# Layer 1 of a channel mixer by seven products of quarters in place of eight, from the fourth chunk on

## The chip, the cores and the metric

One core of one Trainium2 chip. The metric is device microseconds of one execution; the time before is the median of three runs. Engines: PE does matmuls, DVE (VectorE), ACT (ScalarE) and POOL (GpSimd) work elementwise, SP mostly issues DMAs. Each works off its own queue in order.

## The reference

Attention over 32 memory slots for 8 batches x 8 heads, 576 tokens of 64 channels; then a mixer over tokens and one over channels (512 channels, 1536 hidden):

```python
a = exp(phi - max over tokens) ; a /= sum over tokens
k_m, v_m = a^T k, a^T v                      # 32 slots by 64
attn = softmax(q k_m^T / 8)                  # 576 by 32
x    = attn v_m                              # 8 x 576 x 512 after joining the heads
u    = x + (relu(x^T w_tok1) w_tok2)^T       # tokens, d_tok = 256
out  = u + relu(u w_ch1) w_ch2               # channels, d_ch = 1536
```

Products keep float32's accuracy: an operand is split into a high part in the matmul's shorter format (`float32r`, by a cast on ACT) and the rest, the low part (by a subtraction on DVE or POOL), and a product is three matmuls: high x high, high x low, low x high.

## The kernel before

The 8 x 576 rows of `u` are cut into nine *chunks* of 512 columns (columns are tokens here, since everything is held transposed). For a chunk, `u` is 4 groups of 128 channels by 512 columns, in `uh` and `ul`. The hidden layer has 12 blocks of 128 (`f`). Layer 1 of a block, `mm_1`, is 4 channel groups x 3 = 12 matmuls of 512 columns into a PSUM tile `cp` (two of them in turn); then ACT writes the relu's high part (`high`, tile `hh`) and DVE its low part (`low`, tile `hl`). Layer 2 of a block, `ch2`, is 4 output groups x 3 = 12 matmuls into `acc0` to `acc3`, which are summed over all blocks and added to `u` on DVE (`add`), after POOL has put `uh + ul` into `o` (`residual`).

The weights `c1h`, `c1l` (layer 1) and `c2` (layer 2) stay in SBUF for the whole run. After a first part that a planner orders (chunk 0, with the conversion of the weights), the rest is written out as a loop over blocks: each step is layer 1 of block f, then layer 2 of block f-1. Time is counted in half-steps `h`, two a block, 24 a chunk. `at(h, fn)` puts other work at a half-step: heads in sets of four (`Quad(b, Q)`, two a batch), each set with

- `phi_max`, `phi_exp`, `phi_sum` (softmax over tokens), then at `m` `step_kv` (matmuls `kvp`, and small DVE work), `values`,
- at `r+2` `step_s` (matmuls `sp`, then on DVE two transposes, a maximum, a subtraction, and an exp on ACT: `sm1`), at `r+3` `sm2` (sum, reciprocal, product, transpose into `aT` on DVE, then a CAST `a` on ACT, its low part on POOL),
- at `r+6` `nat` and `r+7` `v_pairs` (casts `nat` and four `vv` on ACT, lows on DVE), `r+8` `step_A`, `r+9` `step_R` (token mixer), from `r+10` `step_u` (matmuls `u`, four tiles), whose results go into the chunks' `uh`/`ul`, and for columns of a later chunk into `rest`, from where `take` fetches them.

A step's work on ACT and DVE stands in those engines' queues between the relus of the blocks, in the order in which it is written.

Of the kernel before, what the change touches and what calls it, by code (L numbers as in the profile page):

```python
# [15 lines left out]
ALU = mybir.AluOpType  # L16
# [12 lines left out]
def kernel(  # L29
# [44 lines left out]
    REST = S - CW  # L74

# [34 lines left out]
    c1h = wp.tile([P, NKK, FF], F32R, name="c1h")  # L110
    c1l = wp.tile([P, NKK, FF], F32R, name="c1l")
# [25 lines left out]
    class Chunk:  # L137
        def __init__(s, c):
            s.c, s.n, s.hid = c, f"_{c}", {}
            s.uh = wide(F32R, "uh" + s.n)  # L140
            s.ul = wide(F32R, "ul" + s.n)

# [5 lines left out]
        def mm_1(s, ps, f):  # L148
            w = slice(f * P, (f + 1) * P)
# [10 lines left out]
        def high(s, ps, f):  # L160
            if s.c < CHUNKS - 1 or f < NF - 4:
                h = sb.tile([P, CW], F32R, tag="hh", name=f"hh{f}" + s.n, bufs=2)
                l = sb.tile([P, CW], F32R, tag="hl", name=f"hl{f}" + s.n, bufs=2)
            else:
                if f == NF - 4:
                    s.stay = [
                        sb.tile([P, 4, CW], F32R, tag=t, name="stay" + t, bufs=1)
                        for t in ("rest", "kv")
                    ]
                h, l = (t[:, f - NF + 4] for t in s.stay)  # L170
            s.hid[f] = (h, l)
            relu_high(h, ps)
# [4 lines left out]
        def ch2(s, f):  # L177
            if f == 0:
                s.acc = [
                    pacc.tile([P, CW], F32, tag=f"acc{a}", name=f"acc{a}" + s.n)  # L180
                    for a in range(NKK)
                ]
            s.end = NF - (3 if s.c == CHUNKS - 1 else 0)
            for a in range(NKK):
                s.second(s.acc[a], a, [f], 0, s.end)
# [32 lines left out]

    chunks = {}

    def mixer(c):
        if c not in chunks:
            chunks[c] = Chunk(c)
        return chunks[c]

# [3 lines left out]
    class Quad:  # L229
# [63 lines left out]
        def step_kv(s):  # L293
            s.kvp = pch.tile([P, CW], F32, tag="ch", name="kvp" + s.n)
# [271 lines left out]
        def u_high(s, ps, db, hf):  # L566
# [6 lines left out]
            if n:  # L573
                nc.scalar.copy(out=mixer(s.b).uh[:, kk, to], in_=ps[:, :n])  # L574

        def u_low(s, ps, db, hf):
            kk, (n, to) = 2 * s.Q + db, s.own(hf)
            ch = mixer(s.b)
            if n:
                nc.vector.tensor_tensor(  # L580
                    out=ch.ul[:, kk, to], in0=ps[:, :n], in1=f32(ch.uh[:, kk, to]), op=ALU.subtract
                )
# [112 lines left out]
    class PartC1:  # L695
# [13 lines left out]
        def dst(s):  # L709
            return c1h[:, :, s.w], c1l[:, :, s.w]  # L710
# [874 lines left out]
    beside = {}  # L1585
    for b in range(2, B):
        for Q in range(2):
            qd = second if b == 2 and not Q else Quad(b, Q)
            r = 2 * NF * b - (14 if Q else 26)
            if b == 2 and not Q:  # L1590
                r = m = 2 * NF
            else:

                m = r - (0 if b == 2 else 10 if b > 3 or Q else 8)
                at(max(m - 11, 2 * NF), qd.load_phi)
                at(m - (6 if (b, Q) == (3, 0) else 7), qd.phi_max, k=1)
                at(m - (3 if b == 2 else 4), qd.phi_exp, k=1)
                at(m - (2 if b == 2 else 3), qd.phi_sum, k=1)
                at(loaded + 1, qd.load_kv, k=1)
                at(r - 4, qd.load_q, k=1)  # L1600
            loaded = m
            at(m, qd.step_kv)
            at(m + 4, qd.values)
            if b > 2:
                at(m + 3, qd.get_keys, k=1)
            else:
                at(m + 1, qd.step_T)
            at(r + 2, qd.step_s)
            if Q or b == 2:
                at(r + 3, qd.sm2)  # L1610
            else:
                beside[r + 3] = qd
            at(r + (3 if qd is second else 4), qd.a_pair, 1)
            at(r + 6, qd.nat, k=1)
            at(r + 7, qd.v_pairs)
            at(r + 8, qd.step_A)
            at(r + 9, qd.step_R)
            for x in range(4):
                at(r + 10 + x // 2 * (1 if qd is second else 2), qd.step_u, x // 2, x % 2)
        at(2 * NF * (b - 1) + 7, lambda b=b: mixer(b).take(), k=1)  # L1620
    for c in range(CHUNKS):
        h = 2 * NF * (c + 1)
        if c:
            at(h - (4 if c < CHUNKS - 1 else 8), lambda c=c: chunks[c].residual(), k=1)
        if c == CHUNKS - 1:
            break
        sums = [lambda c=c, x=x: chunks[c].add(x) for x in range(NKK)]
        if h + 1 in beside:
            qd = beside.pop(h + 1)
            sums = [sums[0], qd.S_sum, *sums[1:], qd.S_mul, qd.sm3]  # L1630
        for fn in sums:
            at(h + 1, fn, k=-1)
        at(h + 3, lambda c=c: chunks[c].store(), k=1)
    at(2 * NF * (B - 1) + 7, lambda: mixer(B).take(), k=1)
# [9 lines left out]
    for g in range(NF, NF * CHUNKS):  # L1644
# [6 lines left out]
        if c < CHUNKS - 1 or f < NF - 3:  # L1651
            before[0].ch2(before[1])
# [3 lines left out]
    assert not events and not beside  # L1656

    last = chunks[CHUNKS - 1]
    last.ch2(NF - 4)
# [94 lines left out]
```

## Time and profile before

| | |
|---|---|
| median of 3 runs | 765.95 us (765.69 to 766.15) |
| profiled execution | 765.61 us, span 763.8 us |
| PE / DVE / ACT / POOL busy | 99% / 47% / 32% / 18% of the span |
| granted PE clock | 1.0 throughout |
| HBM | 55.51 MB read, 13.89 MB written, 91 GB/s over the span |

Columns of a row that groups instructions: line, engine, operation, out<-in by the program's names (buffer numbers left out), partitions x elements, count | busy us, mean ns of one | idle time of the engine before them, and what ended it. In order of time: start us, duration us, engine, line, operation. A wait's row: who <- for whom: us in total, times, longest. The busy share of PE says little, since a matmul's listed time overlaps the next one's; distances of starts tell its pace.

### The profile page before, as it was taken

The page shows a single profiled execution, that of the slowest core. Times are in us where ns is not written, and L with a number is a line of the kernel's source. Part 1 is how long each engine was busy: PE and PEld are TensorE (multiplying, and loading weights), DVE is VectorE, ACT ScalarE, POOL GpSimd, SP SyncE. Part 2 cuts the span into 40 slices and gives each one's busy share as a digit, 9 for nine tenths or more (in the row PEclk, how much of TensorE's full clock was granted, in tenths as well). Part 3 has the DMA queues.
Part 4 walks back from the last instruction along what each step waited for, and adds up shares of the span by engine and source line. Part 5 has one row for each costly group of instructions (what it writes and reads, how often), then busy time and mean ns, then how long its engine had stood idle before and what let it go on. Part 6 is the DMA issues. An engine that isn't in the chain of part 4 may idle for free.

```text
span 763.8 us, 11121 instructions
## 1 busy us (share of the span) xinstructions
PE 757.0 (99%) x4514; PEld 631.2 (83%) x4514; DVE 362.3 (47%) x612; ACT 245.2 (32%) x477; POOL 139.8 (18%) x118
## 2 busy tenths in 40 slices
PE   9999999999999999999999999999999999999998
PEld 8777788787878888888888787888888888888886
DVE  4989874657354434545264535543442412212113
ACT  5897553333213231323233221413232312111010
POOL 2144343002311022101310131102310402002000
PEclk9999999999999999999999999999999999999999
DMA  9954630432215040605033220604040101001001
GB/s 357 416 198 157 227 103 10 122 143 65 90 18 192 12 143 1 189 21 154 0 86 123 61 94 15 195 6 149 1 123 0 32 1 56 0 1 56 0 1 55
DMA packets 58178, 70.11 MB, mean 92 GB/s; under 512 B 38416, under 2 KB 48016, under 8 KB 53904
## 3 DMA queue, kind: packets, MB, share of 16 engines
q1 hardware_dynamic: 57696, 68.76, 27.3%
q8 instruction: 35, 0.57, 0.3%
q10 hardware_dynamic: 432, 0.66, 0.2%
q14 instruction: 15, 0.12, 0.1%
HBM read 55.51 MB, written 13.89 MB: 91 GB/s over the span
## 4 chain that ended last, share of the span: by engine, by line
PE 92%; DVE 3%; DMA 2%; ACT 1%; issue 1%; POOL 0%; SPq 0%; ACTq 0%; POOLq 0%
PE cp L158 37%; PE acc L191 36%; PE u L555 8%; PE Ap L515 3%; PE kvp L297 2%; PE u L1213 2%; PE Rp L534 1%; PE sp L393 1%; PE end L191 1%; DMA raww<-in_w_tok_dram 1%; DVE rawc L639 1%; DMA raw<-rows 1%; DVE rawc L622 0%; POOL w1l L650 0%; PE Ap L1188 0%
## 5 line engine op out<-in xcount | busy, mean ns | idle before, releaser
L191 PE MATMUL acc<-hh,c 128*128 128x512 f32 x832 | 276.4, 393 | 0.0
L128 DVE SCALAR_TENSOR_TENSOR hl<-cp,hh 128x512 fp32r<-128x512 f32 x104 | 71.7, 689 | 263.3 <-ACT hh L125 263.2
L191 PEld LDWEIGHTS acc<-hh,c 128*128 128x128 f32 x832 | 156.2, 188 | 37.0 <-issue 4.2
L158 PE MATMUL cp<-uh,c1h 128*128 128x512 f32 x432 | 163.1, 391 | 0.0
L158 PE MATMUL cp<-ul,c1h 128*128 128x512 f32 x432 | 162.4, 390 | 0.0
L191 PE MATMUL acc<-hl,c 128*128 128x512 f32 x416 | 162.3, 390 | 0.0
L158 PE MATMUL cp<-uh,c1l 128*128 128x512 f32 x432 | 162.2, 389 | 0.0
L125 ACT ACTIVATE hh<-cp 128x512 fp32r<-128x512 f32 x104 | 62.0, 596 | 260.8 <-PE cp L158 260.7
L158 PEld LDWEIGHTS cp<-uh,c1l 128*128 128x128 f32 x432 | 81.1, 188 | 17.1
L158 PEld LDWEIGHTS cp<-ul,c1h 128*128 128x128 f32 x432 | 81.1, 188 | 16.4
L158 PEld LDWEIGHTS cp<-uh,c1h 128*128 128x128 f32 x432 | 80.8, 188 | 16.6 <-issue 0.5
L191 PEld LDWEIGHTS acc<-hl,c 128*128 128x128 f32 x416 | 78.2, 188 | 14.1
L203 POOL TENSOR_TENSOR o<-uh,ul 128x512 f32<-128x512 f32 x36 | 48.8, 1383 | 115.3 <-PE cp L158 46.9
L457 POOL TENSOR_TENSOR a<-aT,a 64x576 fp32r<-64x576 f32 x22 | 31.4, 1430 | 183.1 <-ACT a L456 115.9
L456 ACT CAST a<-aT 64x576 fp32r<-64x576 f32 x24 | 16.1, 672 | 56.6 <-DVE aT L430 56.3
L251 DVE TENSOR_REDUCE pr<-phi 128x128 f32<-128x640 f32 x22 | 29.0, 1322 | 10.5 <-ACT phi L275 7.3
L555 PE MATMUL u<-w2l,Rh 128*128 128x288 f32 x112 | 33.1, 295 | 0.0
L555 PE MATMUL u<-w2h,Rh 128*128 128x288 f32 x112 | 33.0, 295 | 0.0
L555 PE MATMUL u<-w2h,Rl 128*128 128x288 f32 x112 | 32.9, 294 | 0.0
L284 POOL PARTITION_ALL_REDUCE psr<-pr x11 | 11.9, 1081 | 88.5 <-issue 56.3
L128 DVE SCALAR_TENSOR_TENSOR Rl<-Rp,Rh 128x512 fp32r<-128x512 f32 x14 | 9.7, 690 | 35.8 <-ACT Rh L125 35.8
L580 DVE TENSOR_TENSOR ul<-u,uh 128x288 fp32r<-128x288 f32 (+8 forms) x48 | 16.9, 356 | 18.9 <-ACT uh L574 18.6
(196 smaller groups left out, 875.1 us busy)
## 6 DMA issues: line engine op xcount, KB each, us to landing
kv<-in_kv_dram SPq DMA_DIRECT2D x12, 1280.0 KB, 6.9
rawc<-in_w_ch_dram SPq DMA_DIRECT2D x12, 1024.0 KB, 10.0
q<-in_q_dram SPq DMA_DIRECT2D x16, 576.0 KB, 5.7
out_dram<-o SPq DMA_DIRECT2D x8, 1024.0 KB, 7.5
phi<-in_phi_dram SPq DMA_DIRECT2D x16, 320.0 KB, 3.8
rows<-S SPq DMA_DIRECT2D x56, 72.0 KB, 2.0
kv<-in_kv_dram SPq DMA_DIRECT2D x6, 640.0 KB, 8.8
raw<-rows SPq DMA_DIRECT2D x14, 256.0 KB, 2.9
```

Source lines behind the costliest of these rows:

```text
L125: nc.scalar.activation(out=h, in_=ps, func=AF.Relu)
L128: nc.vector.scalar_tensor_tensor(out=l, in0=ps, scalar=0.0, in1=f32(h), op0=ALU.max, op1=ALU.subtract)
L158: nc.tensor.matmul(ps, l[:, a, w], r[:, a], start=n == 0, stop=n == len(mm) - 1)
L191: nc.tensor.matmul(ps, l_[f // 2][:, f % 2, a * P : (a + 1) * P], r[:, w], start=f == start and x == 0, stop=f == end - 1 and x == 2,)
L203: nc.gpsimd.tensor_tensor(out=s.o[:, a], in0=f32(s.uh[:, a]), in1=f32(s.ul[:, a]), op=ALU.add)
L251: nc.vector.tensor_reduce(out=m.rearrange("p (i m) -> p i m", i=4), in_=s.pt.rearrange("p i j m -> p i m j"), axis=AX.X, op=op,)
L297: nc.tensor.matmul(s.kvp[32 * i : 32 * i + 32, : 2 * D], s.pt[:, i, j, :], s.kv[:, :, j, i, :], start=j == 0, stop=j == NC - 1,)
L456: nc.scalar.copy(out=h, in_=s.aT[own])
L457: s.low_eng.tensor_tensor(out=l, in0=s.aT[own], in1=f32(h), op=ALU.subtract)
L515: nc.tensor.matmul(ps[:, :TT], a, w, start=x == 0, stop=x == len(mm) - 1)
L555: nc.tensor.matmul(ps[:, :HALF], a, r, start=x == 0, stop=x == len(mm) - 1)
L580: nc.vector.tensor_tensor(out=ch.ul[:, kk, to], in0=ps[:, :n], in1=f32(ch.uh[:, kk, to]), op=ALU.subtract)
```

## The change

Chunks 3 to 8 (`WIN = 3`) do layer 1 by Winograd's form of Strassen's scheme. The 512 channels are cut in two halves, the 512 columns in two (`HW = 256`), and two hidden blocks are taken together (a *pair*): a 2 x 2 by 2 x 2 product of quarters, with seven products in place of eight. One product is 2 channel groups x 3 = 6 matmuls of 256 columns. Six pairs make a chunk; `f` advances by two, four half-steps a pair.

- *Sums of u* (`Quarters`): T1 to T4, four DVE operations of 512 elements a chunk, then highs on ACT and lows on DVE for the seven right sides (`early_1` to `late_4`, in the last 13 half-steps before the chunk). `u` itself stays whole in float32, and the chunk's output is added into it; `residual` falls away.
- *Sums of weights* (`Sums`): in chunks 1 and 2, for each of six pairs, two DVE additions of 512, four of 256, a cast of 1024, a subtraction of 1024; eight DMAs on SP's queue store them with the plain quarters in device memory. In chunks 3 to 8 each pair loads four *units* from there (`load_unit`, on ACT's queue, 512 KB, the fourth 256 KB), two ahead of their use (`AHEAD`). The SBUF of `c1h`, `c1l` becomes twelve tiles for weights, units, sums and results.
- *Products*: two PSUM tiles, `qa` and `qb`, take turns; a sum over products is partly kept in PSUM (T2, T3, T4 go onto what `qa` has), partly made by ACT copies and DVE additions in the tile `c`. After each of the first six products stands a slice of layer 2 of the pair before (three matmuls of 512), after the seventh two.
- The relus: two of 512 on ACT and two on DVE a pair become, on ACT, four copies of 256, two relus of 256 and one of 512; on DVE three additions of 256, two lows of 256 and one of 512.
- The sets of heads come every 12 half-steps, up to six half-steps earlier; the last set ends at half-step 161 of 216. `sm2` of each set stands at `r+3` as one piece (before, it was partly mixed with the chunk's `add`). `kvp` moves from the PSUM pool of `cp` to that of the heads.
- `end`, the last piece of layer 2, has two blocks for three.

```diff
+    HW = CW // 2
+    WIN, AHEAD = 3, 2
...
+        def late_1(s):
+            for name in ("21", "T2", "T3"):
+                s.rooms(name)
+            s.mixed("T3", "22", "12", ALU.subtract)
+            s.mixed("T2", "T3", "11", ALU.add)
+            s.mixed("T4", "21", "T2", ALU.subtract)
+            s.part_high("21", "T2", "T3")
...
+        def product(s, ps, weights, name, first, end):
+            mm = [
+                (l[:, a], r[:, a])
+                for a in range(2)
+                for l, r in (
+                    (weights[:, 0], s.x[name][0]),
+                    (weights[:, 0], s.x[name][1]),
+                    (weights[:, 1], s.x[name][0]),
+                )
+            ]
...
+    def load_unit(n):
...
+        t = sb.tile([P, 1024], F32R, tag="c1", name=f"unit{n}", bufs=NF)
...
+        m = 512 if j == 3 else 1024
+        nc.scalar.dma_start(out=f32(t)[:, :m], in_=sums[p].to[:, j, :m])
...
-            r = 2 * NF * b - (14 if Q else 26)
...
+    starts = [(2, 0, 24, 24), (2, 1, 34, 34), (3, 0, 38, 44), (3, 1, 48, 54), (4, 0, 58, 64)]
+    while starts[-1][:2] != (B - 1, 1):
+        b, Q, m, r = starts[-1]
+        starts.append((b + Q, 1 - Q, r + 4, r + NF))
...
+    for x, h in zip(sums, (4, 9, 14, 24, 29, 34)):
+        for y, fn in enumerate((x.words, x.sum, x.low)):
+            at(2 * NF * (WIN - 2) + h + y, fn, k=1)
...
+        def product(ps, k, name, first):
+            if not k % 2:
+                load_unit(n + k // 2 + AHEAD)
+            ch.product(ps, units[n + k // 2][:, k % 2], name, first, name in ("21", "22", "T4"))
...
+        a = tile("qa")
+        product(a, 0, "11", True)
+        run(h - 1, 1)
+        out(et[:, t0], a)
+        mix()
+        b = tile("qb")
+        product(b, 1, "21", True)
+        add(et[:, t0], b[:, :HW], et[:, t0])
+        run(h, 0)
+        mix()
+        run(h, 1)
+        product(a, 2, "T2", False)
+        out(et[:, t1], a)
+        run(h + 1, -1, 0)
+        mix()
+        product(b, 3, "T1", True)
+        mix()
+        out(ot[:, t0], b)
+        run(h + 1, 1)
+        product(a, 4, "T3", False)
+        out(ot[:, t1], a)
+        add(ot[:, t1], ot[:, t0], ot[:, t1])
+        relu_high(oh[:, t1], ot[:, t1])
+        relu_low(oh[:, t1], ol[:, t1], ot[:, t1])
+        run(h + 2, 0)
+        mix()
+        run(h + 2, 1)
+        product(b, 5, "22", False)
+        add(et[:, t1], b[:, :HW], et[:, t1])
+        relu_high(eh, et)
+        relu_low(eh, el, et)
+        mix()
+        run(h + 3, -1, 0)
+        product(a, 6, "T4", False)
+        relu_high(oh[:, t0], a[:, :HW])
+        relu_low(oh[:, t0], ol[:, t0], a[:, :HW])
+        mix(2)
```

Where the queues stand at the places that matter, in the program's order (names end with batch and set, or with the chunk, and a serial number):

DVE at the softmax of set (5, 1), before: the heads' rows, then the lows of blocks 7 and 8.

```order
L419 TENSOR_REDUCE sm_5_1_4024<-S_5_1_3966 128x18
L420 TENSOR_SCALAR sm_5_1_4024<-sm_5_1_4024 128x18
L421 RECIPROCAL sm_5_1_4024<-sm_5_1_4024 128x18
L424 TENSOR_TENSOR S_5_1_3966<-S_5_1_3966,sm_5_1_4024 128x576
L430 STREAM_TRANSPOSE aT_5_1_4037<-S_5_1_3966 128x576
L128 SCALAR_TENSOR_TENSOR hl7_4_4061<-cp7_4_4045,hh7_4_4060 128x512
L128 SCALAR_TENSOR_TENSOR hl8_4_4095<-cp8_4_4078,hh8_4_4094 128x512
```

The five rows of `sm2` stand ahead of the low part of block 7.

DVE there now (`c1` is the pair's result tile, `qhl13` and `qal12` low parts):

```order
L570 STREAM_TRANSPOSE S_5_1_4296<-sp1_5_1_4287 128x288
L577 TENSOR_REDUCE mx_5_1_4299<-S_5_1_4296 128x18
L580 TENSOR_TENSOR S_5_1_4296<-S_5_1_4296,mx_5_1_4299 128x576
L1851 TENSOR_TENSOR c1_4_4195<-qb1_4_4210,c1_4_4195 128x256
L129 SCALAR_TENSOR_TENSOR qal12_4_4192<-c1_4_4195,qal02_4_4191 128x512
L589 TENSOR_REDUCE sm_5_1_4318<-S_5_1_4296 128x18
L590 TENSOR_SCALAR sm_5_1_4318<-sm_5_1_4318 128x18
L591 RECIPROCAL sm_5_1_4318<-sm_5_1_4318 128x18
L594 TENSOR_TENSOR S_5_1_4296<-S_5_1_4296,sm_5_1_4318 128x576
L600 STREAM_TRANSPOSE aT_5_1_4331<-S_5_1_4296 128x576
L129 SCALAR_TENSOR_TENSOR qhl13_4_4194<-qa1_4_4196,qhh03_4_4193 128x256
```

The heads' rows are the same; the last row, which reads `qa` out, stands behind all of them, as `hl7` did.

ACT at the same place, before:

```order
L125 ACTIVATE hh6_4_3952<-cp6_4_3939 128x512
L415 ACTIVATE S_5_1_3966<-S_5_1_3966 128x576
L456 CAST a0_5_1_4039<-aT_5_1_4037 64x576
L125 ACTIVATE hh7_4_4060<-cp7_4_4045 128x512
L456 CAST a1_5_1_4040<-aT_5_1_4037 64x576
```

The relu of block 7 stands behind the first CAST of `a`.

And now ACT from the softmax to the next pair:

```order
L585 ACTIVATE S_5_1_4296<-S_5_1_4296 128x576
L126 ACTIVATE qal02_4_4191<-c1_4_4195 128x512
L626 CAST a0_5_1_4333<-aT_5_1_4331 64x576
L392 DMA unit33_4337<-sums2_1328 128x1024
L126 ACTIVATE qhh03_4_4193<-qa1_4_4196 128x256
L392 DMA unit34_4359<-sums2_1328 128x1024
```

The relu that reads `qa` comes after the CAST of `a`, as `hh7` did, and after a unit's load.

PE from the seventh product of that pair on (one row per slice or product, x6 for six matmuls):

```order
L327 MATMUL qa1_4_4196<-xT4_4_3988,unit31_4246 128x256 x6
L184 MATMUL acc2_4_4255<-qhh01_4_4027,c20_500 128x512
L184 MATMUL acc2_4_4255<-qhl11_4_4028,c20_500 128x512
L184 MATMUL acc2_4_4255<-qhh01_4_4027,c20_500 128x512
L184 MATMUL acc3_4_4265<-qhh01_4_4027,c20_500 128x512
L184 MATMUL acc3_4_4265<-qhl11_4_4028,c20_500 128x512
L184 MATMUL acc3_4_4265<-qhh01_4_4027,c20_500 128x512
L327 MATMUL qa2_4_4358<-x_4_3556,unit32_4274 128x256 x6
L184 MATMUL acc0_4_4206<-qal02_4_4191,c22_638 128x512
L184 MATMUL acc0_4_4206<-qal12_4_4192,c22_638 128x512
L184 MATMUL acc0_4_4206<-qal02_4_4191,c22_638 128x512
L327 MATMUL qb2_4_4371<-x21_4_3874,unit32_4274 128x256 x6
```

In PSUM the new `qa2` is in the room of `qb1`, and `qb2` in that of `qa1`, so PE waits for the read-out of `qa1` ahead of `qb2`. Before, 24 matmuls of 512 columns stood between layer 1 of a block and the first use of its low part:

```order
L158 MATMUL cp7_4_4045<-ul_4_3107,c1h_98 128x512
L158 MATMUL cp7_4_4045<-uh_4_3106,c1l_99 128x512
L191 MATMUL acc0_4_3699<-hh6_4_3952,c26_852 128x512
L191 MATMUL acc0_4_3699<-hl6_4_3953,c26_852 128x512
L191 MATMUL acc0_4_3699<-hh6_4_3952,c26_852 128x512
```

After the last row of `cp7` come layer 2 of block 6 and layer 1 of block 8, and only then `hl7` is read.

ACT at `nat` and `v_pairs` of that set, before:

```order
L121 CAST nat_5_1_4114<-raw_5_1_4034 128x512
L121 CAST nat_5_1_4114<-raw_5_1_4034 64x128
L465 CAST vv_5_1_4119<-vh_5_1_3736 64x128 x4
L125 ACTIVATE hh9_4_4141<-cp9_4_4124 128x512
L121 CAST Ah_5_1_4160<-Ap_5_1_4145 128x256
```

One relu of a block follows the six casts. ACT there now:

```order
L122 CAST nat_5_1_4464<-raw_5_1_4328 128x512
L122 CAST nat_5_1_4464<-raw_5_1_4328 64x128
L126 ACTIVATE qhh04_4_4353<-c2_4_4357 128x512
L635 CAST vv_5_1_4481<-vh_5_1_4075 64x128 x4
L392 DMA unit37_4486<-sums3_1329 128x1024
L126 ACTIVATE qal05_4_4355<-qa2_4_4358 128x256
```

The four casts of `vv` and a unit's load now stand between two relus of the same pair, and the second of these reads `qa` out.

More of the change, by code (lines that the diff above doesn't have):

```diff
@@ L175, in low, with ch2 @@
             relu_low(*s.hid[f], ps)
[L177 to L184, printed above, removed]
+        def ch2(s, f, channels=range(NKK)):
+            for a in channels:
+                if f == 0 and a == 0:
+                    s.acc = {}
+                if f == 0:
+                    s.acc[a] = pacc.tile([P, CW], F32, tag=f"acc{a}", name=f"acc{a}" + s.n)
                 s.second(s.acc[a], a, [f], 0, s.end)
@@ L1621 @@
-    for c in range(CHUNKS):
-        h = 2 * NF * (c + 1)
[L1623 to L1633, printed above, removed]
@@ L1658 @@
+    for c in range(WIN, CHUNKS):
+        for p in range(NF // 2):
+            quarters(c, p)
+    run(2 * NF * CHUNKS - 1, 1)
+    assert not events
     last = chunks[CHUNKS - 1]
-    last.ch2(NF - 4)
-    for a in range(NKK):
-        last.add(a)
     banks = [(pat, "at", 2)] * 2 + [(pacc, f"acc{a}", 1) for a in range(3)]
```

260 lines of the change are left out of this document (200 added, 60 removed).

## The prediction

> **What bounds the kernel now.** I read the page first (span, busy shares, the chain that ended last), then the waits of PE, then single instructions in order of time, on PE for the pace of a matmul and on DVE and ACT where the heads' softmax falls.
>
> ```profile
> span 763.8 us, 11121 instructions
> PE 757.0 (99%) x4514; PEld 631.2 (83%) x4514; DVE 362.3 (47%) x612; ACT 245.2 (32%) x477; POOL 139.8 (18%) x118
> ...
> PE 92%; DVE 3%; DMA 2%; ACT 1%; issue 1%; POOL 0%; SPq 0%; ACTq 0%; POOLq 0%
> PE cp L158 37%; PE acc L191 36%; PE u L555 8%; PE Ap L515 3%; PE kvp L297 2%; PE u L1213 2%; PE Rp L534 1%; PE sp L393 1%; PE end L191 1%; DMA raww<-in_w_tok_dram 1%; DVE rawc L639 1%; DMA raw<-rows 1%; DVE rawc L622 0%; POOL w1l L650 0%; PE Ap L1188 0%
> ```
>
> PE is the bound: its instructions make 92% of the chain, layer 1 (`cp`) 37% of the span. The two longest waits of PE in the whole run are these; both lie in the first 150 us, and the others are shorter:
>
> ```profile
> PE pp L892 <- POOL mask L89: 1.6, 1, 1.6
> PE pp L943 <- DVE ul L580: 0.5, 1, 0.5
> ```
>
> So the time is the matmuls' pace, as long as nobody makes PE wait. A matmul's listed duration overlaps the next one's; the pace is the distance of starts:
>
> ```profile
> 303.58 0.39 PE L158 MATMUL cp<-uh,c1h 128*128 128x512 f32 x1
> ...
> 304.49 0.39 PE L158 MATMUL cp<-ul,c1h 128*128 128x512 f32 x1
> 758.32 0.28 PE L191 MATMUL end<-staykv,c 128*128 128x256 f32 x1
> ...
> 759.04 0.28 PE L191 MATMUL end<-staykv,c 128*128 128x256 f32 x1
> ```
>
> Four matmuls of 512 columns take 0.91 us, 0.227 each; six of 256 take 0.72 us, 0.120 each.
>
> **Term 1, the seven products.** Per pair of hidden blocks 24 matmuls of 512 (5.45 us) become 42 of 256 (5.04 us): 0.41 us less. Six chunks of six pairs are 36 pairs: **-14.7 us**. An eighth of the columns is gone, but 18 more matmuls each bring some 13 ns that don't shrink (0.120 less half of 0.227, doubled). The Trainium skill ("TensorE: Matmul & The Clock Gate", Back-to-back issue gap) gives N/2.4 + 2.5 ns instead, 216 and 109 ns; by it the term would be -21 us and the sum 6 us lower; the rows disagree with its fixed part, and the measurement decides.
>
> **Where the time goes instead: the room before PE must wait.** In the old order layer 1 of block f is followed by layer 2 of f-1 and layer 1 of f+1, 24 matmuls or 5.45 us, before layer 2 of f needs the relu's low part. The trace uses that room at every softmax:
>
> ```profile
> 506.52 0.72 PE L393 MATMUL sp<-q,kb 64*32 64x288 f32 x16
> 507.17 1.30 PE L297 MATMUL kvp<-kv,phi 128*32 128x128 f32 x40
> 508.40 0.50 PE L191 MATMUL acc<-hh,c 128*128 128x512 f32 x1
> 507.32 0.69 DVE L128 SCALAR_TENSOR_TENSOR hl<-cp,hh 128x512 fp32r<-128x512 f32 x1 [6.42 <-ACT hh L125]
> 507.93 0.84 DVE L400 STREAM_TRANSPOSE S<-sp 128x288 f32<-128x288 f32 x2
> ...
> 509.59 0.76 DVE L410 TENSOR_TENSOR S<-S,mx 128x576 f32<-128x576 f32 x1
> ...
> 512.22 0.73 DVE L419 TENSOR_REDUCE sm<-S 128x18 f32<-128x576 f32 x1
> ...
> 514.29 0.78 DVE L430 STREAM_TRANSPOSE aT<-S 128x576 f32<-128x576 f32 x1
> 516.31 0.69 DVE L128 SCALAR_TENSOR_TENSOR hl<-cp,hh 128x512 fp32r<-128x512 f32 x1 [1.23 <-ACT hh L125]
> 506.69 0.60 ACT L125 ACTIVATE hh<-cp 128x512 fp32r<-128x512 f32 x1 [5.11 <-PE cp L158]
> 510.38 0.69 ACT L415 ACTIVATE S<-S 128x576 f32<-128x576 f32 x1 [3.09 <-DVE S L410]
> 515.11 0.68 ACT L456 CAST a<-aT 64x576 fp32r<-64x576 f32 x1 [4.04 <-DVE aT L430]
> 515.69 0.59 ACT L125 ACTIVATE hh<-cp 128x512 fp32r<-128x512 f32 x1
> ```
>
> ACT reads `cp` 0.17 us after PE moved on (506.69 against 506.52). The next `hh` stands behind the CAST of `a` and starts at 515.69, its `hl` ends at 517.00, and still no wait of PE is listed. In the new order the seventh product's tile `qa` must be read out by ACT and DVE before the *second* product of the next pair may write into it (its first goes into the tile of `qb`, free earlier). Between lie two slices of layer 2, one product and one slice: 1.36 + 0.72 + 0.68 = 2.76 us. And before that reading, in the queues, stand `sm2` on DVE, and the CAST of `a` and a unit's load on ACT (the first two places of the order above).
>
> More durations:
>
> ```profile
> L209 DVE TENSOR_TENSOR o<-end,o 128x256 f32<-128x256 f32 x2 | 0.8, 425 | 1.0 <-PE end L191 1.0
> L122 DVE TENSOR_TENSOR nat<-raw,nat 128x512 fp32r<-128x512 f32 x12 | 8.4, 700 | 12.6 <-ACT nat L121 12.3
> L122 DVE TENSOR_TENSOR nat<-raw,nat 64x128 fp32r<-64x128 f32 x12 | 4.4, 367 | 0.5 <-ACT nat L121 0.2
> L121 ACT CAST Ah<-Ap 128x256 fp32r<-128x256 f32 x12 | 4.5, 372 | 12.6 <-PE Ap L515 12.6
> L465 ACT CAST vv<-vh 64x128 fp32r<-64x128 f32 x48 | 14.2, 296 | 0.4
> L121 ACT CAST nat<-raw 128x512 fp32r<-128x512 f32 x12 | 7.5, 621 | 12.5 <-DMA raw<-rows 12.3
> L121 ACT CAST nat<-raw 64x128 fp32r<-64x128 f32 x12 | 3.5, 294 | 0.6 <-DMA raw<-rows 0.6
> q<-in_q_dram SPq DMA_DIRECT2D x16, 576.0 KB, 5.7
> raw<-rows SPq DMA_DIRECT2D x14, 256.0 KB, 2.9
> L247 SPq DMA_DIRECT2D q<-in_q_dram x14: 328/334/536, 18.6 to 566.2; - x14
> DMA to landing us min/median/max: 3.7/5.7/13.5
> ```
>
> (The last row is that of `q`.) A product is 6 x 0.120 = 0.72 us, a slice (three matmuls of 512) 0.68, `sp` 0.65 (506.52 to 507.17), `kvp` 1.23.
>
> **Term 2, the softmax (`step_s` at r+2, `sm2` at r+3).** Clock 0 is the end of the fifth product. PE itself needs `sp` 0.65, slice, product, slice, product, two slices, product, slice: 6.21 us to the next pair's second product. The queues: copy by ACT 0.17 + 0.37, add on DVE 0.43, half a relu 0.37 and its low part 0.43: 1.77. Transposes to the subtraction (507.93 to 510.35) 2.42: 4.19. Exp 0.69: 4.88, beside it the add of the sixth product. Relu of 512 0.60: 5.48, low part 0.69: 6.17. `sm2` (512.22 to 515.07) 2.85: 9.02. CAST of `a` 0.68: 9.70, issue of the unit 0.33: 10.03, half a relu 0.37 and low part 0.43: 10.83. With 0.04 us at some seven hand-overs (515.07 to 515.11), 11.1. PE waits 11.1 - 6.2 = 4.9 us. Seven sets of heads have their `sm2` in the new chunks (r = 76, 88, ... 148): **+34.3**.
>
> **Term 3, `nat` and `v_pairs` (r+6, r+7), one pair later.** No `sp` here: PE needs 5.56. Copy, add, half a relu 1.34; both casts of `nat` 2.26; DVE has the lows at 2.66 and 3.03, its add at 3.45; relu 4.05; four casts of `vv` 1.18: 5.23; unit 0.33, half a relu 0.37, low part 0.43: 6.36, with hand-overs 6.5. PE waits 0.95, seven times: **+6.7**.
>
> **Term 4, chunk edges.** `late_1` falls right behind `sm2` for three chunks and puts three casts of 0.62 ahead of the copy that the third product waits for: some 0.35 us each, **+1**.
>
> **What costs nothing, and its cover.** A pair without heads' work: from the sixth product's end the add, relu and low part take 0.17 + 0.43 + 0.60 + 0.69 = 1.9 us, needed after 3.5; the seventh product's relu takes 0.17 + 0.37 + 0.43 = 1.0 of 2.76. DVE rises from 1.4 to some 2.8 us a pair, ACT from 1.2 to 2.8 and 1.3 for four issues, of 10.5 us. u's sums and splits (11 of 0.70 on DVE, 7 of 0.62 on ACT a chunk, less the lows of u that fall away) go into such pairs. POOL loses `residual` there, which nobody waited for. Earlier heads leave the last chunks without them: no PE time. Fewer blocks in `end` only move matmuls.
>
> The weights' sums put about 26 us on DVE (6 x (2 x 0.70 + 4 x 0.43 + one of 1024, twice 0.60 to 0.70) = 26) into chunks 1 and 2, and eight DMAs each on SP's queue ahead of `kv`, `q` and `rows`.
>
> ```profile
> 100.00:200.00 100.00, 99.53 (x638) 83.62 (x637) 58.41 (x96) 33.67 (x74) 21.27 (x16) 1.00 0.31 99
> ```
>
> DVE was busy 58 of these 100 us, the room there is the old 5.45, SP is idle most of the time: 0, at most a wait of 1 us at each, 6.
>
> **Units.** Each is 512 KB on ACT's queue. The tightest is issued after the relu behind the sixth product, 1.2 us after it, and needed 5.56 after it: 4.4 us. No row shows such a load; by `q` (576 KB, fastest 3.7) and `raw` (256 KB, 2.9) it lands in some 3.5, by `q`'s median 5.7. `q` shares its queue with `kv` ahead of it, which units don't, so I take 0; the other end is 36 x 1.3 = 47 us. Nothing below zero is possible here, the old kernel had no such loads.
>
> **Sum.** 765.6 (the profiled execution: span 763.8 and 1.8 around it, 0.3 below the median of the runs) - 14.7 + 34.3 + 6.7 + 1.0 = **793**.
>
> **Rivals.**
> - *Faster: the softmax doesn't hold `qa`.* The gain stands and the time is 751. It needs PE's wait for a set of heads to stay under 14.7 / 7 = 2.1 us. Against it: DVE's own rows between `sp` and the second product, 2.42 + 0.43 + 0.69 + 2.85 + 0.43 = 6.8, already pass PE's 5.56 without any of ACT's. For it: that these rows stand one behind the other I read from the order alone, and no run has shown such a wait yet. 13%.
> - *The clock falls in the waits.* PE has no gap like 4.9 us before. At the start, after rest, PE ran slower:
>
> ```profile
> 1.56 4.97 PE L892 MATMUL pp<-ident 128*128 128x128 f32 x30 [1.56 <-POOL mask L89]
> 7.68 2.62 PE L892 MATMUL kp<-ident 128*128 128x128 f32 x22
> ```
>
>   166 ns a matmul against 119: 1.4 us lost over 30. Seven waits would each pay that again: 793 + 10 = 803. The same page of the Trainium skill (Why this matters for your kernels) says that a gap of some 3 us can halve the clock; here only the start bears on it. 20%.
> - *Units land late*, as `q`'s median: 793 + 47 = 840. 7%.
> - *The waits are a third to a half of that*, because PE comes late to these places anyway: 765 to 772. 5%.
>
> My own forecast, 786 to 800, has 55%. The range takes in the clock's case, the six us of the weights' sums, part of the late units and the halved waits: 768 to 822. What this kernel's measurement can tell from no change is about 0.2%, 1.5 us. Faster 0.14 (the first rival and a little of the last), within it 0.03, slower 0.83.
>
> **What the new profile would show.** Matmuls of `qa` and `qb` 0.120 us apart. PE's waits lead with `qb` on DVE's low part of the relu, seven times near 5 us, between some 400 and 700 us; ACT's CAST of `a` just ahead of the half relu; the chain with DVE and ACT well above 3% and 1%; the last two chunks without waits. If `qa` or `qb` waits on DMA of `unit` in nearly every pair, the units' term is wrong; if PE's waits sum to less than 15 us, Term 2 is.

## The result, and the profile after

The changed kernel takes 821.08 us, median of 4 runs (819.54 to 821.39), against 766.05 for the one before beside it: a ratio of 1.0715, 95% interval 1.0697 to 1.0734. It is 55 us slower; 27 were forecast. The profiled execution took 819.54 us, its span is 817.8, its mean granted clock 0.979.

The page's head, and the chain that ended last:

```profile
span 817.8 us, 13215 instructions
PE 771.7 (94%) x5159; PEld 660.4 (81%) x5159; DVE 469.7 (57%) x840; ACT 322.7 (39%) x699; POOL 110.5 (14%) x94
...
PE 41%; DMA 9%; DVE 7%; ACT 3%; issue 1%; SPq 0%; ACTq 0%; DVEq 0%
```

The shares are of the whole span, but this chain can be followed back only to 307 us, so they add up to 62%. Of that part PE makes about two thirds (41 of 62), DMA a seventh, DVE a ninth; before, the chain reached back to the start and PE made 92% of it. So DMA, DVE and ACT have come onto the path. PE's busy 94% hides part of that, since matmuls at half the clock count as busy for twice as long. PE's waits (who waits <- for whom: us in total, times, longest), the longest rows, that of the start left out:

```profile
PE qb L327 <- DVE qhl L129: 24.5, 7, 3.6
PE qa L327 <- DMA unit<-sums: 5.8, 6, 1.7
PE qb L327 <- DVE qal L129: 3.3, 7, 0.5
...
PE acc L184 <- DVE qal L129: 1.0, 6, 0.2
PE acc L184 <- DVE hl L129: 0.8, 1, 0.8
```

The first is Term 2, seven times; the third Term 3. The first of the seven in order of time (start us, duration us, engine, line, operation; [idle before <- releaser]), from the end of the fifth product:

```profile
327.96 0.72 PE L563 MATMUL sp<-q,kb 64*32 64x288 f32 x16
...
331.38 0.76 DVE L580 TENSOR_TENSOR S<-S,mx 128x576 f32<-128x576 f32 x1
...
333.41 0.69 DVE L129 SCALAR_TENSOR_TENSOR qal<-c,qal 128x512 fp32r<-128x512 f32 x1 [0.94 <-ACT qal L126]
333.62 1.27 PE L184 MATMUL acc<-qal,c 128*128 128x512 f32 x3
334.02 0.74 DVE L589 TENSOR_REDUCE sm<-S 128x18 f32<-128x576 f32 x1
...
336.10 0.78 DVE L600 STREAM_TRANSPOSE aT<-S 128x576 f32<-128x576 f32 x1
336.92 0.67 ACT L626 CAST a<-aT 64x576 fp32r<-64x576 f32 x1 [3.54 <-DVE aT L600]
337.49 0.37 ACT L126 ACTIVATE qhh<-qa 128x256 fp32r<-128x256 f32 x1
337.90 0.42 DVE L129 SCALAR_TENSOR_TENSOR qhl<-qa,qhh 128x256 fp32r<-128x256 f32 x1 [1.02 <-ACT qhh L126]
338.38 0.58 PE L327 MATMUL qb<-x,unit 128*128 128x256 f32 x1 [3.49 <-DVE qhl L129]
```

PE is done with the slice of layer 2 at 334.89 and stands still until 338.38. All that time the half relu that reads `qa` (337.49) waits behind the CAST, and the CAST behind `sm2` on DVE.

What came on top is the clock. Busy time in seven stretches just after these waits began (us: busy and count of PE, PEld, DVE, ACT, POOL; granted PE clock; DMA share; GB/s):

```profile
337.10:343.90 6.80, 5.52 (x50) 4.52 (x51) 2.75 (x10) 1.81 (x4) 2.81 (x2) 0.50 0.87 236
388.30:391.70 3.40, 3.40 (x38) 2.73 (x27) 2.51 (x7) 2.08 (x4) 0.55 (x1) 0.50 1.04 331
...
630.60:637.40 6.80, 5.14 (x19) 4.16 (x18) 0.39 (x1) 0.37 (x1) 1.07 (x1) 0.50 0.60 192
sum 34.00, PE 30.32 PEld 24.94 DVE 16.33 ACT 8.95 POOL 9.30; mean PE 4.33 PEld 3.56 DVE 2.33 ACT 1.28 POOL 1.33
```

Each wait of 3.5 us is followed by one stretch of 3.4 or 6.8 us at half the clock. PE was busy in 30.3 of these 34 us; at half rate half of that is lost, some **15 us** by this estimate. Two runs below bear out the half. The same pair, with the same 87 matmul records, has one stretch of 3.4 us and a wait of 2.97 us in the spread version, and neither of them with the units three ahead (the same columns, of the first and then of the second):

```profile
478.80:496.50 17.70, 14.73 (x87) 13.11 (x86) 10.27 (x19) 6.15 (x17) 1.24 (x1) 0.90 0.61 228
```

```profile
474.35:487.29 12.94, 12.94 (x87) 11.90 (x86) 10.47 (x19) 6.17 (x17) 1.24 (x1) 1.00 0.96 357
```

PE's work took 1.8 us more, for a stretch of 3.4. In the changed kernel the set of `kvp` behind the first wait shows the clock in one row, 2.36 us where 40 of them took 1.30 before:

```profile
339.96 2.36 PE L467 MATMUL kvp<-kv,phi 128*32 128x128 f32 x40
```

And the gain, in the last chunks, where no heads' work is left. Starts of the same matmul in two pairs, of after and then of before:

```profile
713.48 0.88 PE L327 MATMUL qa<-x,unit 128*128 128x256 f32 x6
724.02 0.88 PE L327 MATMUL qa<-x,unit 128*128 128x256 f32 x6
```

```profile
643.28 0.39 PE L158 MATMUL cp<-uh,c1h 128*128 128x512 f32 x1
654.16 0.39 PE L158 MATMUL cp<-uh,c1h 128*128 128x512 f32 x1
```

10.54 us a pair against 10.88: 0.34 less, and no wait of PE in all of these pairs but one of 0.5.

The books of the profiled execution (819.5 against 765.6, +53.9):

| part | forecast | measured |
|---|---|---|
| Term 1, seven products | -14.7 | 36 x -0.34 = -12.2 |
| Term 2, softmax | +34.3 | +24.5 |
| Term 3, `nat`, `v_pairs` | +6.7 | +3.3 |
| Term 4, `late_1` | +1 | no wait of its own above 0.4 |
| units | 0 | +5.8 |
| weights' sums, earlier heads | 0 (to +6) | +2.9, +3.1 (from the runs below) |
| half clock | only as a rival, +10 | +15 |
| layer 2 on the relus' lows, and the like | 0 | +2.3 |

That is +45. Of the other 9, 1.2 lie ahead of the first layer 1 (and differ by as much between runs of kernels alike there). The two runs below that free PE of its waits for units have spans 7.5 and 8.3 us shorter, where these waits are 5.8: some 2 more of the 9 go with the units. Part of the rest lies in gaps of under 0.35 us, at slices of layer 2 above all; it wasn't taken apart.

### The profile page after: what moved, and what is told of

It is laid out like the page before. It is cut to its first block, busy times and chain, and to the rows that moved or that the text cites. A ratio compares the mean times of both kernels' runs of the same rounds, so it can differ in the third digit from the quotient of the medians.

```text
span 817.8 us, 13215 instructions
## 1 busy us (share of the span) xinstructions
PE 771.7 (94%) x5159; PEld 660.4 (81%) x5159; DVE 469.7 (57%) x840; ACT 322.7 (39%) x699; POOL 110.5 (14%) x94
## 4 chain that ended last, share of the span: by engine, by line
PE 41%; DMA 9%; DVE 7%; ACT 3%; issue 1%; SPq 0%; ACTq 0%; DVEq 0%
PE acc L184 17%; PE qa L327 9%; PE qb L327 8%; DMA unit<-sums 6%; PE u L725 4%; DMA raw<-rows 2%; DMA rows<-S 2%; PE kvp L467 1%; DVE c L1851 1%; ACT qal L126 1%; DVE S L570 1%; PE end L184 1%; PE Rp L704 1%; DVE qal L129 1%; DVE S L580 1%
## 5 line engine op out<-in xcount | busy, mean ns | idle before, releaser
L184 PE MATMUL acc<-qhh,c 128*128 128x512 f32 x376 | 144.7, 395 | 0.0
L327 PE MATMUL qb<-x,unit 128*128 128x256 f32 x648 | 98.1, 288 | 27.8 <-DVE qhl L129 24.5
L327 PEld LDWEIGHTS qa<-xT,unit 128*128 128x128 f32 x648 | 93.1, 192 | 18.1 <-ACT vh L506 4.3
L327 PE MATMUL qa<-xT,unit 128*128 128x256 f32 x648 | 96.0, 284 | 5.8 <-DMA unit<-sums 5.8
L184 PE MATMUL acc<-hh,c 128*128 128x512 f32 x288 | 96.9, 396 | 0.0
L184 PEld LDWEIGHTS acc<-hh,c 128*128 128x128 f32 x288 | 54.1, 188 | 14.8 <-issue 4.0
L184 PE MATMUL acc<-hl,c 128*128 128x512 f32 x144 | 56.3, 391 | 0.8 <-DVE hl L129 0.8
L161 PE MATMUL cp<-uh,c1h 128*128 128x512 f32 x144 | 51.0, 394 | 0.0
L161 PE MATMUL cp<-ul,c1h 128*128 128x512 f32 x144 | 50.3, 390 | 0.0
L161 PE MATMUL cp<-uh,c1l 128*128 128x512 f32 x144 | 50.2, 389 | 0.0
```

The lines of the kernel that those rows point to most:

```text
L161: nc.tensor.matmul(ps, l[:, a, w], r[:, a], start=n == 0, stop=n == len(mm) - 1)
L184: nc.tensor.matmul(ps, l_[f // 2][:, f % 2, a * P : (a + 1) * P], r[:, w], start=f == start and x == 0, stop=f == end - 1 and x == 2,)
L327: nc.tensor.matmul(ps[:, :HW], l, r, start=first and n == 0, stop=n == len(mm) - 1, skip_group_check=not first,)
```

## The experiments

Theory: PE waits because one PSUM tile is read out late, its reader standing behind the softmax in two queues; the waits bring the clock down; the rest is units, sums and heads. Rivals: the order isn't what matters (another reading would be late instead), and the half clock has some other cause. Every ratio is to the kernel before.

**Read-out first.**

```diff
-        run(h + 3, -1, 0)
         product(a, 6, "T4", False)
         relu_high(oh[:, t0], a[:, :HW])
         relu_low(oh[:, t0], ol[:, t0], a[:, :HW])
+        run(h + 3, -1, 0)
         mix(2)
```

> sm2 and v_pairs are called behind the read-out of the seventh product instead of ahead of it; the work is the same. Theory: of the 55 us, 28 are PE's seven waits for that read-out (24.5 + 3.3) and about 17 the seven stretches at half the granted clock (34 us in all) that begin inside the long waits. Both go: 821 - 28 - 17 = 776, clock 1.000. Rival A: the half clock comes from something else in the changed chunks (twice the DMA traffic, shorter matmuls): only the waits go, 793, clock still about 0.98. Rival B: the wait moves to the third product of the next pair, whose copy on ACT now stands behind sm2 and the CAST: by the rows some 5.3 us after the seventh product's end against PE's 4.2 (5.4 where kvp lies between), so up to 1 us each: 776 to 783.

810.35 us, ratio 1.0571 [1.0547, 1.0594]: beyond the theory and both rivals. In kind it is rival B, since the waits moved. The clock was 0.989, 17 us at half for 34. The 28 us of waits were gone from `qb` and stood elsewhere:

```profile
PE qa L327 <- DVE c L1851: 11.7, 7, 2.9
PE qa L327 <- ACT c L1848: 10.4, 7, 2.3
PE qa L327 <- DMA unit<-sums: 9.6, 8, 2.4
```

One is the copy behind the CAST, as rival B had it; the other I hadn't seen coming. `nat` still stands at r+6, but PE, which no longer stands still for 3.5 us, gets there sooner, while `sm2` sends its rows to memory no earlier in the pair (3.5 us after the pair's first product began, 3.2 in the changed kernel). So the casts of `nat` wait for them at the head of ACT's queue:

```profile
442.96 0.82 ACT L122 CAST nat<-raw 128x512 fp32r<-128x512 f32 x2 [3.13 <-DMA raw<-rows]
443.61 1.01 DVE L123 TENSOR_TENSOR nat<-raw,nat 128x512 fp32r<-128x512 f32 x2 [3.32 <-ACT nat L122]
444.65 0.43 DVE L1851 TENSOR_TENSOR c<-qb,c 128x256 f32<-128x256 f32 x1
445.13 1.11 PE L327 MATMUL qa<-x,unit 128*128 128x256 f32 x6 [2.42 <-DVE c L1851]
```

A wait for DMA on ACT becomes one on DVE and then one of PE. Moving one piece of a chain moved the wait.

**The wait filled with work.**

```diff
+        if h in [r + 4 for _, _, _, r in starts]:
+            load_unit(n + AHEAD)
+            for _ in range(6):
+                ch.product(a, units[n][:, 0], "11", True, False)
+        else:
             product(a, 0, "11", True)
```

> In the seven pairs behind a softmax the first product is computed six times over (each starts anew, so only the last counts): 30 matmuls more, 30 x 0.119 = 3.6 us of work on PE in the place of the 3.5 us wait. PE's idle time turns into work, nothing gets shorter. Theory (the idle time lowers the clock): the 24.5 us of waits become 25 us of work, the half clock goes, 821 - 17 = 804, clock 1.000. Rival (the half clock has another cause): 821, clock 0.98.

823.09 us, ratio 1.0745 [1.0727, 1.0763]; clock 0.993. As a time it looks like the rival. The trace says otherwise: two stretches at half clock were left (10 us for 34), and the filler made waits of its own, since the copy of the first product stands behind it:

```profile
PE qa L327 <- DMA unit<-sums: 8.1, 8, 1.5
PE qa L327 <- DVE c L1851: 7.8, 6, 1.8
PE qb L327 <- DVE qal L129: 2.6, 5, 0.5
PE qb L327 <- DVE qhl L129: 2.3, 7, 0.4
```

In the new chunks the waits fell by 13 us, the filler adds 25 and 24 us less at half clock give back some 10: +2; +3.8 were measured between the two spans. So idle time that became work took most of the half clock with it. The two stretches that stayed follow waits of 1.8 us for `c`, the longest left. One thing stays open: the other executions of this kernel had clocks of 1.000, 0.991 and 0.998 and times of 822.45 to 823.71, so that a stretch seems to have cost less there than half of its length.

**Products without units' loads.**

```diff
-        t = sb.tile([P, 1024], F32R, tag="c1", name=f"unit{n}", bufs=NF)
+        t = w1h.rearrange("p c t -> p (c t)")[:, :1024]
...
-        nc.scalar.dma_start(out=f32(t)[:, :m], in_=sums[p].to[:, j, :m])
```

> The seven products take their weights from a tile that stays in SBUF: the 144 loads of units and their 67 MB fall away (the sums are still made and stored; the output is not the reference's). It prices the units: PE's 5.8 us of waits on them, one issue of 0.33 us ahead of each read-out on ACT, and the pace of the 512-column matmuls in the new chunks, 0.233 us against 0.227 before. Theory: waits 5.8 gone, seven softmax waits 0.3 shorter (2.3), pace unchanged, half clock stays: 821 - 8 = 813. Rival (the DMA writes slow the matmuls): 860 x 0.006 = 5 us more, 808, and 0.227 in the rows. Rival (the DMA traffic is what lowers the clock): 813 - 17 = 796 with clock 1.000.

811.56 us, 1.0599 [1.0581, 1.0618]: the theory's 813, within its runs (810.54 to 813.50). The seven long waits are the same, and so is the clock, so the DMA traffic isn't what lowers it:

```profile
PE qb L327 <- DVE qhl L129: 24.5, 7, 3.6
PE qb L327 <- DVE qal L129: 3.2, 7, 0.5
```

The waits did not shrink by the issue of a load, as I had reckoned: an issue on ACT lies beside the CAST ahead of it. The 512-column matmuls kept 0.233, and an undisturbed pair 10.54.

**Units three ahead.**

```diff
-    WIN, AHEAD = 3, 2
+    WIN, AHEAD = 3, 3
```

> The units' loads are issued one unit (two products) earlier: three ahead for two. Theory: PE's waits for units (5.8 us in 6 places, each where the issue stood late on ACT) go, nothing else changes: 821 - 6 = 815, or 813 where the read-outs behind also come sooner. Rival: the loads wait for a free tile instead and hold ACT's queue, with the read-outs behind them: 825 or more.

811.49 us, 1.0599 [1.0581, 1.0617]: all of what taking the loads away brings. PE's waits for units are gone from the list. Issued one unit earlier, the same bytes cost no wait. In the changed kernel the six loads that PE waited for took 5.0 to 7.3 us to land, where the median is 4.3. By the medians both runs gain 9.5 us, more than the 5.8 of waits.

**Old layer 1 everywhere, with sums and earlier heads; then the heads alone.**

```diff
-    WIN, AHEAD = 3, 2
+    WIN, AHEAD = CHUNKS, 2
...
-            at(2 * NF * (WIN - 2) + h + y, fn, k=1)
+            at(2 * NF + h + y, fn, k=1)
```

The second leaves out the last line; both put back the old end of the last chunk. In the first the remainder of `u` for a chunk is fetched six half-steps late, when its tile already holds the next batch's, so it adds up other numbers; the operations are the same.

> Layer 1 in the old form in all nine chunks; the weights' sums by way of memory and the earlier heads stay as in the changed kernel. It prices what the prediction put at 0 to 6 us. Theory: the sums' DVE rows and DMAs cost small waits in chunks 1 and 2; the trace of the changed kernel comes 9.1 us later to the first of the seven products, of which 1.2 are there from the start and about 2.1 are one more set of kvp and sp done by then, so 5 to 6 us remain: 766 + 1.2 + 5.5 = 772 to 773, clock 1.000. Rival (they only shift work, all of it given back in the last chunks): 766. Rival (earlier heads cost by themselves in the later chunks too): above 776.

> Layer 1 in the old form in all chunks and no weights' sums at all; the heads start as early as in the changed kernel. It splits the 10.6 us that the run with old layer 1 in all chunks lay over the kernel before. Theory: the sums carry most of it: their 26 us of DVE rows and their 48 DMAs stand in chunks 1 and 2 among the heads' work. Heads alone then cost 2 us: 768. Rival: the earlier heads cost it (the sets 10 blocks apart fall on top of each other's steps in chunks 1 and 2): 774 to 776.

776.52 us, 1.0136 [1.0119, 1.0153], and 770.11 us, 1.0054 [1.0039, 1.0069]. The first has a wait of its own that the changed kernel doesn't show:

```profile
PE sp L571 <- DVE ul L224: 2.9, 3, 2.6
```

and 3.4 us at half clock behind it; without these 4.3 it would be the theory's 772, though the time as it is lies with the second rival (above 776). My forecast for the heads alone was half of what they cost. At the last block of chunk 2, matmuls done earlier or later taken off, PE is late against the kernel before by 4.2 us with the heads alone (1.1 of it from the start) and by 7.2 in the changed kernel (1.2 from the start): the earlier heads cost 3.1, the sums 2.9. Neither stands in one big wait; the longest of PE in those chunks of the changed kernel is 0.8.

**Halves of the PSUM tiles in turn.**

```diff
+    halves_of = {}
...
-            return pch.tile([P, CW], F32, tag="ch", name=f"{x}{p}" + ch.n, bufs=2)
+            if x not in halves_of:
+                halves_of[x] = pch.tile([P, CW], F32, tag="ch", name=x, bufs=2)
+            return halves_of[x][:, p % 2 * HW : (p % 2 + 1) * HW]
```

> The order stays as in the changed kernel; only the tiles of the seven products are doubled. A product of 256 columns fills half of a tile of 512; pairs now take the left and the right halves of both tiles in turn, so the second product of the next pair no longer writes where the seventh still has to be read. Theory: it was that reading alone that held PE. The 24.5 + 3.3 us of waits go; in their place the third product of the next pair waits for ACT's copy of the first, which the trace of the changed kernel shows 2.96 us after PE fell idle (334.92 to 337.88, and 0.37 long): PE gets there after 0.72 + 1.3 + 0.7 + 0.72 + 0.7 = 4.1, so no wait or a few tenths. Without long waits the clock stays up: 821 - 28 - 17 = 776, clock 1.000. Rival A: writing one half while the other half of the same tile is read is ordered as before, or costs as much: 821. Rival B (as behind the run with the read-out first): the softmax's 2.9 us on DVE and its casts on ACT hold some other reading instead, 2 to 3 us each: 795 to 808.

842.13 us, 1.0994 [1.0978, 1.1011], clock 0.967: slower than any. Rival A, and worse:

```profile
PE qa L327 <- DVE qhl L129: 41.0, 10, 5.4
PE qa L327 <- DVE qal L129: 13.0, 7, 1.9
```

By these rows the program orders a write behind the readings of the whole tile, and now the *first* product of the next pair (`qa`) goes into the tile that is read last; it is needed one product and one slice sooner (1.4 us), and the wait is 1.8 longer (5.4 against 3.6). So this run agrees with how the wait is said to be made up, but what separate halves would bring wasn't tried.

**The softmax's pieces spread.** Read-out first, and besides:

```diff
-            s.a_pair(0)
...
-        at(r + (3 if qd is second else 4), qd.a_pair, 1)
-        at(r + 6, qd.nat, k=1)
-        at(r + 7, qd.v_pairs)
...
+        n = 2 if b > 3 else 0
+        for p in range(2):
+            at(r + (3 if qd is second else 4), qd.a_pair, p)
+        at(r + 6 + n, qd.nat, k=1)
+        at(r + 7 + n, qd.v_pairs)
```

(`step_A`, `step_R` and `step_u` also come `n` later.)

> The read-out of the seventh product goes ahead of sm2 as in the first run; besides, the first CAST of a moves from sm2 to the place of the second (r+4, behind the copy that the third product needs), and nat, v_pairs and the steps behind them come two blocks later (from batch 4 on), since in the first run the casts of nat stood at the head of ACT's queue waiting for raw (3.1 us) with the copies behind them. Same work. Theory: what was left in the first run were two waits for each set of heads, 1.5 us at the third product (copy behind the CAST) and 1.7 us behind nat: both go, 0.3 to 0.5 us stay at the second product: 810 - 22 + 3 - 8 for the half clock = 783, clock 1.000. Rival: the softmax finds another reading to hold, 2 us each: 795 to 805.

784.47 us, 1.0242 [1.0182, 1.0301], clock 0.993. The theory's number: 37 us of the 55 are given back by order alone. What is left:

```profile
PE qa L327 <- DMA unit<-sums: 9.6, 4, 4.0
PE qa L327 <- ACT c L1849: 4.1, 3, 1.4
```

and the clock falls behind the two longest of these waits only.

**And the units three ahead.** (The spread softmax, `AHEAD` 3.)

> The spread softmax with the units three ahead. Theory: what is left in the spread kernel's trace are 9.6 us of waits for units in 4 places and 4.1 us for ACT's copy in 3 (there late_1 casts three quarters of u ahead of it), with 10 us at half clock in two places, both behind a wait for a unit (2.1 to 4.0 us). With units ahead: 784.5 - 9.6 - 5 = 770, clock 0.999. Rival: the units come late because their issue stands behind ACT's casts, and one more ahead only halves it: 777.

773.93 us, 1.0116 [1.0099, 1.0133], clock 1.0 in the profiled execution (0.997 to 0.999 in the others). That is 10.5 less where 14.5 were expected, about midway between the theory's 770 and the rival's 777: one wait for a unit (2.0) stayed, and the rest of the difference wasn't found.

**`early` and `late` quarters one block later.**

```diff
-                (-13, "early_1"), (-12, "early_2"), (-5, "late_1"), (-4, "late_2"),
+                (-12, "early_1"), (-11, "early_2"), (-4, "late_1"), (-3, "late_2"),
```

> As the run before it, and early_1, early_2, late_1, late_2 one block later, which puts their casts behind the copy that the third product needs. Theory: the 4.1 us of waits for that copy go: 766, the time before the change. Rival: the casts hold the next reading instead: 770.

779.64 us, 1.0189 [1.0169, 1.0209]: the rival, and beyond its 770. The wait for the copy grew from 4.1 to

```profile
PE qa L327 <- ACT c L1849: 7.7, 4, 2.4
```

since the casts, which wait for `late_1`'s additions on DVE, still stand in one piece ahead of a copy, only of another (that for the fifth product in place of the third).

**And the sums' additions on POOL.** (`nc.gpsimd` for `nc.vector` in `words` and `sum`.)

> As the run before it, and the weights' additions (words and sum; not the splits) on POOL instead of DVE. Old layer 1 with the sums lay 6.4 us above the same heads without them. Theory: DVE's rows of the sums stand ahead of relu's low parts and of the splits of u in chunks 1 and 2; 6 x 6 additions of 0.4 to 0.7 us leave DVE, about 18 of 26 us, so some two thirds of the 6.4 go: 762. Rival: POOL is slower at them (a residual of 512 columns is 1.4 us by the planner's cost in the code against DVE's 0.7), the sums reach memory later, and heads' work on POOL waits: 766 or more.

810.44 us, 1.0581 [1.0567, 1.0596], clock 0.983: the rival, 31 us slower than the run before it. The additions of 512 take 1.33 us each on POOL (0.68 on DVE), and `sum` ends in a cast on ACT that waits for them with everything behind it:

```profile
PE Ap L684 <- ACT nat L122: 20.0, 4, 11.7
```

**Casts two blocks behind their additions, units four ahead.** (On the spread softmax: `part_high` moves from `early_1` and `late_1` into `early_2` and `late_2`, which come at -11 and -3, ahead of the block's other work.)

> The spread softmax with units four ahead, and early and late quarters split: their additions on DVE stay where they were, their casts on ACT come two blocks later, behind the copy that the third product needs. Theory: 4.1 us (copy behind casts that wait for DVE) and 2.0 us (one unit) of the 774 go: 768, no half clock. Rival: as one block later, the casts only hold the next reading: 774 to 780.

770.09 us, 1.0057 [1.0040, 1.0074], the best version. Two things change at once here, so their shares stay open. No wait in the new chunks is over 1.3 us, and the clock is full:

```profile
PE qb L327 <- DVE c L1852: 2.0, 3, 0.7
PE pp L1061 <- POOL mask L91: 1.6, 1, 1.6
PE acc L184 <- DVE hl L129: 1.3, 1, 1.3
```

From the pair behind the first softmax to the end of the seven sets of heads, 21 pairs, it takes 288.7 us (331.69 to 620.34); the changed kernel takes 338.4 (332.91 to 671.32). These 49.8 are nearly all of the 51 us between the two. The first product of these 21 pairs and the first behind them, here and then in the changed kernel:

```profile
331.69 0.40 PE L327 MATMUL qa<-x,unit 128*128 128x256 f32 x2
620.34 0.40 PE L327 MATMUL qa<-x,unit 128*128 128x256 f32 x2
```

```profile
332.91 0.28 PE L327 MATMUL qa<-x,unit 128*128 128x256 f32 x1
671.32 0.40 PE L327 MATMUL qa<-x,unit 128*128 128x256 f32 x2
```

**And the sums' steps farther apart.** (Steps two half-steps apart instead of one, at 4, 10, 16, 22, 28, 34.)

> As the run before it, with the three steps of each weights' sum two half blocks apart, behind layer 2 instead of two of three ahead of relu's low part. Theory: of the 6 us that chunks 1 and 2 cost, 2.8 belong to the sums (7.2 against 4.2 us late at the end of chunk 2 for the same heads without sums, start included) and most of that goes: 2 us below the run before it, 766. Rival: they fall on other heads' steps there: no change or slower.

779.46 us, 1.0174 [1.0161, 1.0187]: the rival. On DVE a chunk's `add` now stands behind a sum's four additions, and these behind a head's rows that wait 3.1 us for POOL; layer 2 of the next chunk waits for the `add`:

```profile
PE acc L184 <- DVE o L202: 4.0, 1, 4.0
```

Behind this wait, and behind two of 1.4 and 1.7 some 53 us later, PE ran 10 us in all at half clock.

No version is faster than the kernel before. The span of the best one is 3.0 us longer: the pairs give 12 us, PE comes 4.8 late to the end of chunk 2 and waits 4 in the new chunks. That makes -3; some 6 more weren't taken apart.

## Why the prediction was right or wrong

*Direction, and the mechanism of Term 2:* right. The wait predicted as Term 2 leads PE's list, at the place in the program, on the instruction and the number of times named (in time from 335 to 626 us, where I had written 400 to 700), and reordering around it gives most of the time back. The faster rival (the softmax doesn't hold `qa`) is out.

*The size:* wrong, 55 for 27. The step that failed is the sum: it takes PE's waits at full clock, and puts the units, the weights' sums and the earlier heads at nothing. In the order of what they cost:

- **The clock** was a rival at 20% and not a term of the sum. It belonged into the sum: with the waits of Term 2 it came with every one of the seven. Its price was taken from the start of the kernel, 1.4 us each; in the profile it is 15 / 7 = 2.1. The two stand or fall together, so that a forecast of seven waits of several us with an unharmed clock was not the likeliest case. The Trainium skill ("TensorE: Matmul & The Clock Gate", Why this matters for your kernels), which I had weighed, warns of gaps from some 3 us; the seven waits of 3.5 agree, and shorter ones, most of them of 1.8 to 2.9, brought the clock down as well in some of the runs. In the expectations of the first two runs I took half of 34 us, 17; part of these stretches PE was still waiting.
- **Costed at nothing:** units (+5.8 of waits; the cover was reckoned for a load that lands in 3.5, and the median is 4.3, and 5.0 to 7.3 in the six places where PE waited), weights' sums (+2.9, within the bound of 6) and earlier heads (+3.1, for which I had written "no PE time"), layer 2's waits for lows and the like (+2.3). Together 14; the two runs without waits for units put the units nearer to 8.
- **Term 2** was 10 too high. The chain from the fifth product's end was forecast at 11.1 and took 10.4 (327.96 to 338.38): its rows up to the end of `sm2` came within 0.1 (8.92 for 9.02), but the issue of the unit cost nothing and the hand-overs were already in the rows. PE's own way was forecast at 6.2 and took 6.9 (to 334.89): `sp` took 0.64 as forecast, but the slice behind it 0.81, and the last slice, which waits some 0.4 for the low part of `qal`, 1.27 to its listed end, where 0.68 each were reckoned. 0.7 on both sides makes 3.5 for 4.9.
- **Term 3**: 0.5 for 0.95. Without the issue of the unit (0.33) and the hand-overs (0.14) its sum comes out at that.
- **Term 1**: 0.34 a pair for 0.41. The matmuls of 256 were as forecast (0.118 for 0.120). The first two matmuls of 512 behind them start 233 and 236 ns apart instead of 227, so that a slice of three takes 0.697 instead of 0.681, eight times a pair.
- **Term 4**: no wait of its own; its place mattered only once the other waits were gone (4.1 us in the spread version).

The terms that were off (-9.8, -3.4 and -1, and Term 1's +2.5) nearly cancel those costed at nothing (+14), so that the miss of 27 is mostly the clock's 15 and the 9 that no term names, of which some 2 go with the units.

## What to carry to other kernels

A wait of PE costs more than its length once it is long enough to bring the clock down: put both into one term. A step that computes less but needs each result read out sooner is worth what its longest reader in the queues leaves of it; list for every product what stands ahead of its reader on ACT and DVE, casts that wait for a DMA or another engine above all, before counting matmuls. And when such a wait is moved by reordering, ask which instruction is now behind the piece that was moved: three of the runs here (the read-out first, the quarters one block later, the sums' steps farther apart) moved a wait rather than removing it.

## What the runs showed of the hardware

- The granted clock fell in whole stretches of 3.41 or 6.83 us, 1.9 to 4.9 us after a wait of 3.5 us began, and every such wait was followed by one (seven of seven in the changed kernel, and again seven of seven in each of two more runs, without the units' loads and with the units three ahead). The starts of the seven stretches lie 14 or 15 times 3.41 us apart (337.06, 388.26, 436.05, 483.83, 531.62, 582.82, 630.61). The Trainium skill ("TensorE: Matmul & The Clock Gate", What's actually happening) has a free-running window of 3413 ns; the lengths here are one and two of them.
- Shorter waits did it too, but not always: with the read-out first, four of seven waits of 2.0 to 2.9 us; with the quarters one block later, one of three of 2.4, and besides one of 1.2; in the filled kernel, two of nine of 1.2 to 1.8. In the spread version with the units three ahead, three of 1.4 and one of 2.0 didn't.
- A matmul of 512 columns is slower right behind those of 256 (233 and 236 ns for the first two of a slice, against 227 in the kernel before), with and without the units' DMA traffic.
